# Order and due times of the row scatters in a planned attention and mixture-of-experts kernel

## The chip, the cores and the metric

The kernel runs on one core of one Trainium2 chip. The metric is device time in microseconds (us), the median of three runs.

## The reference

Eight batches of eight heads, 576 tokens, head size 64, with a causal window of 128 and a linear bias per head; then a mixture of eight experts on the 4608 resulting tokens (512 wide, 1024 hidden), each token going to one expert.

```
scores = q @ k.T / 8 + slope[h] * -|i - j|      where 0 <= i - j < 128, else -1e9
x      = (softmax(scores) @ v)                  -> (4608, 512)
logits = (x / |x|) @ (emb / |emb|).T / tau
e      = argmax(logits);  g = softmax(logits)[e]
out    = g * (relu(x @ w1[e]) @ w2[e])
```

## The kernel before, in words

**Two stages.** `attention` makes the tokens tile by tile, and `moe` runs the experts. There are 36 tiles of 128 query rows: per pair of batches eight tiles of one batch (a `first` one, which has no earlier tile, and three `full` ones, for each of the two batches) and one `pair` tile with the last 64 rows of both. Each tile is done in two halves of four heads, so that there are 72 half tiles, u = 0 to 71.

**A half tile** goes through TensorE (`score`, L595 and L616), VectorE (`merge` L626, `max` L633), ScalarE (`exp` L640), TensorE again (`flip`, a transpose, L648), ScalarE and VectorE (`phi` L494 and `plo` L497, which split the probabilities into two 16-bit parts), GpSimd (`mask`, two or three selects, L668 and L681; none in a `first` tile), TensorE (`av`, L700 and L716) and VectorE (`recip` L732, `norm` L738). A tile then has `xhi` (L752 or L754), `xlo` (GpSimd, L765), a transposing DMA of SyncE (`xdma`, L769), `logit` (L775, L779) and `lcopy` (L788). `v_lo` (L570) is a further GpSimd job per tile.

**Routing.** `GROUPS` is 8, 8, 8, 6, 4, 2 tiles. When the last tile of a group has its logits, a chain of some 20 small operations, nearly all on VectorE (`route`, L843 to L865), finds each token's expert and its row there (`di`); `mark` writes the token's number and weight beside it (L876); and `put`, an indirect DMA of GpSimd (L880, L881), scatters a tile's 128 rows of 514 words from the tile `gx` into the table `xs` in HBM. There are 13 `gx` buffers (`XBUFS`), so that tile T + 13 can be written only when tile T is scattered.

**The head start.** After the third group (`GP` = 2, 24 tiles) the expert that has most tokens is chosen (`head_ops`, L336 to L343). Its weights come in 16 pieces (`fetch` L927) that ScalarE and VectorE split (`whi` L930, `wlo` L934), its first 384 rows come from `xs` (`head_rows`, L941 and L945, which wait for the 24 scatters), and TensorE computes them between the attention's jobs (`hid` L962, `out` L986). `y` (L993 on ScalarE, L995 on VectorE) and `yput` (GpSimd, L998 and L396) store the result.

**The hand-over.** After the last group `count_ops` (L354 to L357) read how many tokens the head expert has in all, and `rank_ops` (L376 to L389) order the others. In `moe`, `blank_rows` (L1285) writes zeros from `zrow` behind an expert's last token, and `rows` (L1302, L1307, L1314) reads the expert's tokens from `xs` by a transposing DMA, which waits for all 36 scatters. `hidden` (L1391), `hidden_part`, `output` (L1435), `scaled` and `put` (L396) follow, expert by expert in the order of `TURNS`.

**Who sets the order.** The class `Plan` holds jobs with an engine, an assumed length in ns, what they come after, which buffers they take, and a due time. It gives each engine's next place to the job with the earliest due among those that can start within `SLACK` of the earliest start (400 ns on GpSimd); jobs marked `fill` come last. The due time of a stage of half tile u is 2800 u plus a constant (`STEP`, `DUE`): 5600 for `mask`, 16700 for `put`. The result is a fixed order of instructions on each engine, and on the chip an engine takes them in that order. An `ORDER` dependency only sets the order and makes nothing wait on the chip.

Of the kernel before, what the change touches and what calls it, by code (L numbers as in the profile page):

```python
# [39 lines left out]
GP = 2  # L40
# [128 lines left out]
def kernel(  # L169
# [156 lines left out]
    def head_ops(z):  # L326
# [5 lines left out]
        def ke(nm):  # L332
# [10 lines left out]
            ("DVE", 90, lambda: V.tensor_copy(k1("he", I32), k1("hf"))),  # L343
            ("SP", 500, lambda: head_box["start"]()),
        ]

    def count_ops(z):
        V = nc.vector

        def ke(nm):  # L350
            return kt_(nm, [P, E])

        return [
            ("DVE", 90, lambda: V.tensor_copy(ke("cnt"), z["cnt"])),  # L354
            ("DVE", 90, lambda: V.tensor_tensor(ke("hn"), ke("ho"), ke("cnt"), op=ALU.mult)),
            ("DVE", 90, lambda: V.tensor_reduce(kt_("n0", [P, 1]), ke("hn"), axis=AX.X, op=ALU.add)),
            ("DVE", 90, lambda: V.tensor_copy(kt_("n0i", [P, 1], I32), kt_("n0", [P, 1]))),  # L357
        ]

    def rank_ops(z):  # L360
# [42 lines left out]
    def attention(actx):  # L403
# [386 lines left out]
        def route_ops(gi):  # L790
# [47 lines left out]
            def ids():  # L838
# [22 lines left out]
                *(count_ops(z) if tail else []),  # L861
# [32 lines left out]
        def route_kinds(gi):  # L894
            G, tail = groups[gi], gi == len(groups) - 1
            o = [("DVE", 70), ("ACT", 100), ("ACT", 100)] + [("DVE", 70)] * 6 + [("DVE", 135)] * 7
            o += [("PE", 40 * G + (40 * G if tail or gi == GP else 0))]
            o += [("DVE", 90)] if gi == GP else []
            o += [("DVE", 90)] * 4 if tail else []
# [51 lines left out]

        def head_hidden(ft, c):
# [37 lines left out]
        def head_y(a):  # L990
            hd["y", a] = y = stg.tile([P, DM], F32, tag="stg", name=f"y_head_{a}")
            if a % 2:
                nc.scalar.activation(y, hd["ps2", a], AF.Copy, scale=hd["gs"][:, a : a + 1])  # L993
            else:
                nc.vector.tensor_scalar(y, hd["ps2", a], hd["gs"][:, a : a + 1], None, op0=ALU.mult)  # L995
# [45 lines left out]
        for T in range(NT):  # L1041
# [3 lines left out]
            for n in "kq":  # L1045
                if T >= 2:
# [9 lines left out]
                    f"turn_{n}{T}", "PE", 470 + SWITCH, lambda a=key: prep_pe(a[1], a[0]),  # L1056
# [20 lines left out]
            for hf in range(2):  # L1077
# [5 lines left out]
                    f"score{u}", "PE", (640 if first else 980 if pair else 960 if t % 2 else 1180) + 150, lambda a=a: score_pe(*a),  # L1083
# [4 lines left out]
                for j in range(2):  # L1088
# [16 lines left out]
                    f"flip{u}", "PE", 452 + SWITCH, lambda a=a: probs_pe(*a), after=[f"exp{u}_0", (f"exp{u}_1", -230)],  # L1105
# [16 lines left out]
                    f"av{u}", "PE", (490 if first else 1190 if pair else 842) + SWITCH, lambda a=a: values_pe(*a),  # L1122
# [16 lines left out]
                f"xhi{T}", "DVE" if dv else "ACT", 335 if dv else 520, lambda T=T: x_act(T),  # L1139
# [34 lines left out]
        for gi, G in enumerate(groups):  # L1174
# [6 lines left out]
            for i, (e, ns) in enumerate(kinds[0]):  # L1181
                dep = list(prev)
                if i == R_RANK and gi:
                    dep.append(f"total{gi - 1}")
                J(
                    f"route{gi}_{i}", e, ns, of(gi, 1, i), after=dep, due=due("route", u) + 150 * i,
# [10 lines left out]
            for g in range(G):  # L1197
# [5 lines left out]
                    f"put{T0 + g}", "POOL", 1030, of(gi, 3, g), land=1000, moves=700, after=[done, f"mark{T0 + g}", f"xlo{T0 + g}"], uses=[("gx", T0 + g)],  # L1203
                    due=due("put", u) + 1500 * g,
# [8 lines left out]
            if tail:  # L1213
                prev = [done]
                for i, (e, ns, f) in enumerate(rank_ops({})):
                    J(f"order{i}", e, ns, f, after=prev, due=due("route", u) + 150 * (i + 30))
                    prev = [f"order{i}"]
# [3 lines left out]
        for i in range(NP):  # L1221
# [4 lines left out]
            J(f"wlo{i}", "DVE", 602, lambda i=i: part_lo(i), after=[f"whi{i}"], uses=[("stg", i)], due=d + 5500, fill=True)  # L1226
        J("head_rows", "SP", 5500, head_rows, land=1500, moves=5000, after=[f"put{T}" for T in range(GT)] + [started], due=due("put", u) + 12000)
        J("head_info", "DVE", 150, head_info, after=["head_rows"], due=1e7)
# [10 lines left out]
        for a in range(HEAD // P):  # L1239
# [6 lines left out]
            J(f"y{a}", "ACT" if a % 2 else "DVE", 600, lambda a=a: head_y(a), after=[f"out{a}_5", "head_info"] + [f"fetch{i}" for i in range(NP)], makes=[("stg", ("y", a))], uses=[("ps2", a)], due=2e7)  # L1246
            J(f"yput{a}", "POOL", 1200, lambda a=a: head_put(a), after=[f"y{a}"], uses=[("y", a)], due=3e7)
# [9 lines left out]
    def moe(mctx):  # L1257
# [18 lines left out]
        def blank_rows(s):  # L1276
            (nb, hb), b0 = blocks(s), first_row(s) // P
            if s == 0:
                e = head_box["e"]
            else:  # L1280
                e = nc.sync.value_load(ebi[0:1, s : s + 1], min_val=0, max_val=E - 1)
            nt = sel_["n0i"][0:1, 0:1] if s == 0 else nki[0:1, s : s + 1]
            n = nc.sync.value_load(nt, min_val=0, max_val=NTOK)
# [8 lines left out]
            if s == 0:  # L1292
                state[s].update(w1=(w["w1h"], w["w1l"]), w2=(w["w2h"], w["w2l"]))
# [184 lines left out]
        for p, s in enumerate(TURNS):  # L1478
# [5 lines left out]
                f"blank{s}", "SP", 5.9 * ((nb - b0) * P + hb), lambda s=s: blank_rows(s), due=lead - 3000, early=handed["order"],  # L1484
# [3 lines left out]
                f"rows{s}", "SP", 7.0 * (SLOTS[s] - b0 * P) + 600, lambda s=s: rows(s), after=[(f"blank{s}", 2000)], early=handed["rows"],  # L1488
# [200 lines left out]
```

## Time and profile before

| what | us |
|---|---|
| median of three runs | 671.62 |
| lowest and highest of them | 667.55, 672.62 |
| the profiled execution, its own time | 668.15 |
| its span, first to last instruction | 666.4 |
| TensorE busy in the span | 629.3 |
| VectorE, ScalarE, GpSimd busy | 388.4, 331.3, 262.6 |
| mean granted TensorE clock | 0.985 |

The span is what the profile's rows divide up; 1.75 us of the execution's time lie around it. Matmuls are pipelined and their ends are modelled, so that a busy TensorE is not one at its peak. Times in rows count from the start of the span. The attention fills the span up to about 297 us, the experts the rest.

### The profile page before, as it was taken

Reading aid. Unit: us, or ns where it says so; the run is one execution under the profiler, and the core shown is the slowest. Engines: PE = TensorE matmul, PEld = TensorE weight load, DVE = VectorE, ACT = ScalarE, POOL = GpSimd, SP = SyncE. Lnnn points to the kernel's source line nnn. Section 1 sums busy time; section 2 is a strip of 40 time slices with the busy share of each in tenths; the row PEclk is TensorE's granted clock in tenths of the full one; section 3 lists DMA queues with packets and bytes.
Section 4 is the critical chain, followed back from the end, with each engine's and each line's share of the span. In section 5 each row is a group of like instructions: output and inputs, shape, how many; then the busy total and the mean of one; then the engine's idle time right before and its main releaser. Section 6 shows DMA issues by size and latency. Waiting matters only on the chain. (4 is left out here: it accounts for less than half of the span.)

```text
span 666.4 us, 15711 instructions
## 1 busy us (share of the span) xinstructions
PE 629.3 (94%) x6043; PEld 423.5 (64%) x6043; DVE 388.4 (58%) x989; ACT 331.3 (50%) x777; POOL 262.6 (39%) x472
## 2 busy tenths in 40 slices
PE   7999989989999998989989999999999999999993
PEld 4887767767877775636555585574674855754442
DVE  5988869997999999732356336245352364310250
ACT  5999777878877895302265225243332253210200
POOL 7677588779668656730110301011102012002011
PEclk9999999999988997999999999999999999999998
DMA  9998979988969993459999917807729264001000
GB/s 194 197 203 171 184 202 158 183 195 198 189 128 272 208 212 96 137 157 221 242 319 281 326 69 158 272 33 199 262 61 303 95 168 156 2 16 48 12 32 32
DMA packets 217676, 109.83 MB, mean 165 GB/s; under 512 B 195829, under 2 KB 195829, under 8 KB 217600
## 3 DMA queue, kind: packets, MB, share of 16 engines
q1 hardware_dynamic: 211760, 89.89, 61.2%
q0 software_dynamic: 5840, 18.92, 7.6%
q8 instruction: 48, 0.79, 0.5%
q14 instruction: 28, 0.23, 0.1%
HBM read 61.92 MB, written 28.12 MB: 135 GB/s over the span
## 5 line engine op out<-in xcount | busy, mean ns | idle before, releaser
L1391 PE MATMUL ps<-xT,w1h 128*128 128x272 f16 (+7 forms) x896 | 173.5, 293 | 5.2 <-DMA xT<-xs 3.2
L1391 PE MATMUL ps<-xT,w1l 128*128 128x272 f16 (+7 forms) x448 | 131.5, 293 | 0.0
L396 POOL DMA_INDIRECT out_dram<-y,ids x32 | 35.0, 1095 | 204.9 <-DVE y L1449 96.0
L1391 PEld LDWEIGHTS <-w1h 128*128 128x128 f16 x896 | 87.6, 98 | 35.9 <-issue 5.9
L1399 DVE SCALAR_TENSOR_TENSOR hl<-ps,hh 128x272 f16<-128x272 f32 (+7 forms) x112 | 51.5, 474 | 95.6 <-ACT hh L1401 95.6
L1435 PE MATMUL ps<-w2h,hl 128*128 128x512 f16 (+1 forms) x264 | 98.4, 373 | 1.4 <-DVE hl L1399 1.4
L1435 PE MATMUL ps<-w2h,hh 128*128 128x512 f16 (+1 forms) x264 | 98.4, 373 | 0.0
L1435 PE MATMUL ps<-w2l,hh 128*128 128x512 f16 (+1 forms) x264 | 98.4, 373 | 0.0
L1401 ACT ACTIVATE hh<-ps 128x272 f16<-128x272 f32 (+7 forms) x112 | 45.6, 425 | 101.7 <-PE ps L1391 92.2
L640 ACT ACTIVATE pe<-sc,nm 128x128 f32<-128x128 f32 x288 | 85.6, 390 | 12.9 <-DVE nm L633 9.9
L1435 PEld LDWEIGHTS <-hh 128*128 128x128 f16 x528 | 51.4, 98 | 58.6 <-issue 0.8
L616 PE MATMUL sc<-kh,qh 64*128 64x128 f32 (+2 forms) x768 | 69.8, 328 | 0.8 <-ACT qh L494 0.8
L494 ACT ACTIVATE pq<-ptp 128x512 f16<-128x512 f32 x72 | 55.1, 765 | 14.7 <-PE ptp L648 13.7
L616 PEld LDWEIGHTS sc<-kh,qh 64*128 64x128 f32 (+1 forms) x768 | 55.1, 183 | 9.2 <-issue 4.8
L497 DVE SCALAR_TENSOR_TENSOR pq<-ptp,pq 128x512 f16<-128x512 f32 x72 | 52.8, 733 | 11.5 <-ACT pq L494 11.0
L1366 DVE SCALAR_TENSOR_TENSOR w2l<-ws,w2h 128x1024 f16<-128x1024 f32 x28 | 33.8, 1223 | 38.0 <-ACT w2h L1368 37.7
L633 DVE TENSOR_REDUCE nm<-sc 128x2 f32<-128x256 f32 x144 | 55.2, 413 | 0.4 <-PE sc L616 0.3
L1366 DVE SCALAR_TENSOR_TENSOR w1l<-ws,w1h 128x1024 f16<-128x1024 f32 x28 | 33.4, 1221 | 37.0 <-ACT w1h L1368 36.8
L648 PE MATMUL ptp<-ident,pe 128*128 128x128 f32 x288 | 47.9, 288 | 5.7 <-ACT pe L640 2.2
L1391 PEld LDWEIGHTS <-w1l 128*128 128x128 f16 x448 | 43.8, 98 | 14.4
L1368 ACT ACTIVATE w2h<-ws 128x1024 f16<-128x1024 f32 x28 | 29.1, 1054 | 43.2 <-DMA ws<-moe_w_dram 41.0
L1368 ACT ACTIVATE w1h<-ws 128x1024 f16<-128x1024 f32 x28 | 28.4, 1052 | 44.1 <-DMA ws<-moe_w_dram 44.1
(231 smaller groups left out, 1203.9 us busy)
## 6 DMA issues: line engine op xcount, KB each, us to landing
ws<-moe_w_dram SPq DMA_DIRECT2D x56, 512.0 KB, 9.9
ldk<-k_dram SPq DMA_DIRECT2D x32, 256.0 KB, 4.5
ldq<-q_dram SPq DMA_DIRECT2D x32, 256.0 KB, 5.0
ldv<-v_dram SPq DMA_DIRECT2D x32, 256.0 KB, 4.2
stg<-moe_w_dram SPq DMA_DIRECT2D x16, 256.0 KB, 4.6
xs<-zrow SPq DMA_DIRECT2D x3, 1092.2 KB, 9.2
xs<-zrow SPq DMA_DIRECT2D x1, 1413.5 KB
xs<-zrow SPq DMA_DIRECT2D x1, 1285.0 KB
```

The source lines that it names most:

```text
L494: nc.scalar.activation(hi, ps, AF.Copy, scale=scale)
L497: nc.vector.scalar_tensor_tensor(lo, ps, scale, hi, op0=ALU.mult, op1=ALU.subtract)
L616: nc.tensor.matmul(sc[T, hf, j][o, l, w], qT[T]["h"][rows, hp, o], at["h"][rows, hp, kc], start=False, stop=True, skip_group_check=True,)
L633: nc.vector.tensor_reduce(nm_t[T, hf, j], sc[T, hf, j][:, :, 0:P], axis=AX.X, op=ALU.min)
L640: nc.scalar.activation(pr_t[T, hf][:, 2 * l + j, :], ps[:, l, 0:P], AF.Exp, bias=nm[:, l : l + 1], scale=-1.0)
L648: nc.tensor.transpose(pt[:, i, :], pe[:, i, :], ident)
L1366: nc.vector.scalar_tensor_tensor(lo_, x, SW, hi, op0=ALU.mult, op1=ALU.subtract)
L1368: nc.scalar.activation(hi, x, AF.Copy, scale=SW)
L1391: nc.tensor.matmul(ps[:, :w], a[:, kt, fs], xx[:, b + kt, c0 : c0 + w], start=(n == 0), stop=(n == len(jobs) - 1))
L1399: nc.vector.scalar_tensor_tensor(hl[:, ft, c0 : c0 + w], ps[:, :w], 0.0, hi, op0=ALU.max, op1=ALU.subtract)
L1401: nc.scalar.activation(hi, ps[:, :w], AF.Relu)
L1435: nc.tensor.matmul(ps, x[:, ft, a * P : (a + 1) * P], w[:, ft, c], start=(n == 0), stop=(n == len(jobs) - 1))
```

## The change

The due time of the scatters is new. For the first two groups it is the due time of the mask just before tile T + 13 needs the buffer; for the third it is that of the masks 58 to 65; for the last three groups it lies behind all masks, and they also come after `head_blank`. `head_blank` is a new job of SyncE that writes the zero rows of the head expert behind its count after the third group, so that the late scatters write over them; `count_ops` and the first `blank_rows` are gone, and `head_ops` has one more cast (`hmi`). The copy of the counts that opened `count_ops` is now the first of `rank_ops`. `yput` comes after the last scatter in GpSimd's order, and all three `y` are on ScalarE. Many assumed lengths in the plan are set anew.

```diff
+            ("DVE", 90, lambda: V.tensor_copy(k1("hmi", I32), k1("hm"))),
-    def count_ops(z):
...
+            ("DVE", 90, lambda: V.tensor_copy(ke("cnt"), z["cnt"])),
-                *(count_ops(z) if tail else []),
+        def head_blank():
+            n = nc.sync.value_load(sel_["hmi"][0:1, 0:1], min_val=HEAD, max_val=NTOK)
+            m = (SLOTS[0] + 31) // 32 * 32 - HEAD
+            d = nc.sync.dma_start(
+                xs[ds(hd["e"], 1), ds(n, m), :].rearrange("o (a p) c -> p (o a) c", p=32),
+                zrow[0:32].unsqueeze(1).to_broadcast([32, m // 32, ROW]),
+            )
+            for p_ in scatters:
+                tc.declare_no_dep(d.ins, p_.ins, reason="rows beyond the expert's tokens")
         def head_y(a):
-            if a % 2: nc.scalar.activation(...)
-            else: nc.vector.tensor_scalar(...)
+            nc.scalar.activation(y, hd["ps2", a], AF.Copy, scale=hd["gs"][:, a : a + 1])
-  turn, flip  "PE", 470 + SWITCH, 452 + SWITCH
+  turn, flip  "PE", 470 + SWITCH // 2, 452 + SWITCH // 2
-  score  (640 if first else 980 if pair else 960 if t % 2 else 1180) + 150
+  score  (960 if first else 1078 if pair else 1185 if t % 2 else 1212) + SWITCH
-  av     (490 if first else 1190 if pair else 842) + SWITCH
+  av     (500 if first else 1720 if pair else 870) + SWITCH // 2
-  xhi    335 if dv else 520
+  xhi    400 if dv else 535
-  route  ns
+  route  ns + (45 if e == "DVE" else 0)
-  wlo    602
+  wlo    750
-  J(f"put{T0 + g}", "POOL", 1030, ..., after=[done, f"mark{T0 + g}", f"xlo{T0 + g}"],
-    due=due("put", u) + 1500 * g)
+  J(f"put{T0 + g}", "POOL", 1270, ..., after=[...] + (["head_blank"] if gi > GP else []),
+    due=due("mask", 2 * (T0 + g + XBUFS) - 2) if gi < GP else due("mask", u + 11 + g) if gi == GP
+        else due("mask", 2 * NT) + 1e4 + 100 * g)
+  J("head_blank", "SP", 1300, head_blank, land=1500, moves=2300,
+    after=[started] + [(f"put{T}", ORDER) for T in range(GT)] + then("score", 2 * NT - 8),
+    due=due("put", u) + 20000)
-  J(f"y{a}", "ACT" if a % 2 else "DVE", 600, ...)
-  J(f"yput{a}", "POOL", 1200, lambda a=a: head_put(a), after=[f"y{a}"], ...)
+  J(f"y{a}", "ACT", 600, ...)
+  J(f"yput{a}", "POOL", 1200, lambda a=a: head_put(a), after=[f"y{a}", (f"put{NT - 1}", ORDER)], ...)
   def blank_rows(s):
       if s == 0:
-          e = head_box["e"]
+          state[s] = dict(e=head_box["e"], ...); return
-  J(f"rows{s}", ..., after=[(f"blank{s}", 2000)], ...)
+  J(f"rows{s}", ..., after=[(f"blank{s}", 2000 if s else ORDER)], ...)
```

## Rows read from the trace of the kernel before

**Rows 1.** The profile's page, part 1: busy time, share of the span and instructions of each engine.

```profile
PE 629.3 (94%) x6043; PEld 423.5 (64%) x6043; DVE 388.4 (58%) x989; ACT 331.3 (50%) x777; POOL 262.6 (39%) x472
```

**Rows 2.** Busy time in stretches: the stretch, its length, then busy us and instructions of PE, PEld, DVE, ACT and POOL, the granted clock, the DMA share and GB/s.

```profile
30.00:70.00 40.00, 40.00 (x612) 32.28 (x608) 33.72 (x97) 35.77 (x98) 30.41 (x44) 1.00 1.00 184
90.00:100.00 10.00, 7.62 (x98) 5.77 (x98) 4.74 (x14) 7.52 (x22) 9.04 (x16) 1.00 0.91 259
150.00:160.00 10.00, 8.53 (x143) 6.73 (x140) 7.73 (x21) 7.90 (x25) 9.63 (x15) 1.00 0.87 229
190.00:200.00 10.00, 8.88 (x110) 6.78 (x106) 9.90 (x39) 6.46 (x17) 6.92 (x21) 0.83 0.51 110
210.00:220.00 10.00, 8.39 (x102) 6.67 (x100) 9.07 (x21) 7.78 (x20) 7.93 (x13) 0.83 1.22 234
240.00:258.00 18.00, 14.76 (x229) 11.34 (x226) 18.00 (x57) 15.19 (x42) 11.05 (x14) 0.99 0.76 150
260.00:270.00 10.00, 10.00 (x89) 6.45 (x86) 8.45 (x23) 4.50 (x13) 8.23 (x15) 0.78 0.35 132
```

**Rows 3.** TensorE in order of time: the first matmuls of the scores of half tiles u = 6, 18, 24, 36, 48, 54 and 66. Columns: start, length, engine, line, what it writes and reads.

```profile
26.12 0.39 PE L595 MATMUL sc<-brow,bcol 64*128 64x512 bf16 x2
...
64.20 0.38 PE L595 MATMUL sc<-tab_first,identb 128*128 128x256 bf16 x2
...
85.46 0.39 PE L595 MATMUL sc<-brow,bcol 64*128 64x512 bf16 x2
...
128.16 0.38 PE L595 MATMUL sc<-tab_first,identb 128*128 128x256 bf16 x2
...
170.96 0.39 PE L595 MATMUL sc<-brow,bcol 64*128 64x512 bf16 x2
...
190.92 0.38 PE L595 MATMUL sc<-tab_first,identb 128*128 128x256 bf16 x2
...
236.06 0.39 PE L595 MATMUL sc<-brow,bcol 64*128 64x512 bf16 x2
```

**Rows 4.** GpSimd in order of time, the first group's scatters: the first and the sixth, and the first selects of the masks of half tiles 22 and 23 behind them.

```profile
86.72 1.18 POOL L881 DMA_INDIRECT xs<-gx,di  x1 [1.06 <-DVE nm L633]
...
93.27 0.96 POOL L881 DMA_INDIRECT xs<-gx,di  x1 [0.19 <-issue]
94.25 0.64 POOL L668 TENSOR_SCALAR_AFFINE_SELECT md<-pq 128x512 f32<-128x512 f32 x1
...
97.95 0.64 POOL L668 TENSOR_SCALAR_AFFINE_SELECT md<-pq 128x512 f32<-128x512 f32 x1
```

**Rows 5.** VectorE in order of time: the `plo` of half tiles 22, 23 and 70, each the last thing that its mask needs.

```profile
86.67 0.75 DVE L497 SCALAR_TENSOR_TENSOR pq<-ptp,pq 128x512 f16<-128x512 f32 x1
...
89.39 0.72 DVE L497 SCALAR_TENSOR_TENSOR pq<-ptp,pq 128x512 f16<-128x512 f32 x1
...
263.61 0.74 DVE L497 SCALAR_TENSOR_TENSOR pq<-ptp,pq 128x512 f16<-128x512 f32 x1
```

**Rows 6.** TensorE in order of time: the `av` that uses the mask of 94.25 us, with its wait in brackets.

```profile
94.94 0.21 PE L716 MATMUL av<-vh,md 128*128 128x65 f16 x1 [1.22 <-POOL md L668]
```

**Rows 7.** The scatters and the split of the head's weights (shortest, median and longest ns, first and last start), and two rows of the list of DMA issues (KB each and us from issue to landing, where given).

```profile
L881 POOL DMA_INDIRECT xs<-gx,di x36: 957/963/1182, 86.7 to 290.1; - x36
...
L934 DVE SCALAR_TENSOR_TENSOR w1l<-stg,w1h x8: 676/756/2341, 209.7 to 230.3; 128x512 f16<-128x512 f32 x8
...
xs<-zrow SPq DMA_DIRECT2D x1, 578.2 KB, 4.5
xs<-gx,di POOLq DMA_INDIRECT x36, 5.4
```

**Rows 8.** The last rounds of the attention, in order of time on GpSimd, VectorE, SyncE and TensorE: the first select of mask 70; the head's first `yput`; the last scatter; the copy of the counts (the first of `count_ops`), the head's first `y` and the last group's rows `di`; the blank rows of the head expert and the first `rows`; the head's last matmul and the experts' first.

```profile
269.65 0.90 POOL L681 TENSOR_SCALAR_AFFINE_SELECT tails<-pq 64x256 f32<-64x256 f32 x2
...
287.54 1.00 POOL L396 DMA_INDIRECT out_dram<-y_head,ids_head  x1 [1.29 <-DVE df L864]
...
290.11 0.96 POOL L881 DMA_INDIRECT xs<-gx,di  x1 [0.19 <-issue]
...
285.70 0.14 DVE L354 COPY cnt<-ptr 128x8 f32<-128x8 f32 x1
...
286.51 0.75 DVE L995 TENSOR_SCALAR y_head<-ps_head,gs_head 128x512 f32<-128x512 f32 x1
...
287.68 0.17 DVE L865 CAST di<-df 128x2 int32<-128x2 f32 x1
...
287.34 0.38 SPq L1285 DMA_DIRECT2D xs<-zrow  x1
295.33 2.26 SPq L1302 DMA_TRANSPOSE xT<-xs  x1
...
296.45 0.38 PE L986 MATMUL ps_head<-w2h,hl_head 128*128 128x512 f16 x1
300.07 0.40 PE L1391 MATMUL ps<-xT,w1h 128*128 128x288 f16 x2 [3.23 <-DMA xT<-xs]
```

**Rows 9.** SyncE and TensorE in order of time: the read of the head expert's rows, a load for the last tile, and the head's first matmuls.

```profile
228.30 4.20 SPq L941 DMA_TRANSPOSE x_head<-xs  x1
...
242.07 1.32 SPq L428 DMA_DIRECT2D ldq<-q_dram  x2
...
243.30 0.49 PE L962 MATMUL ps_head<-x_head,w1h 128*128 128x384 f16 x2
```

More of the change, by code (lines that the diff above doesn't have):

```diff
@@ L1202, in attention @@
                 J(
-                    f"put{T0 + g}", "POOL", 1030, of(gi, 3, g), land=1000, moves=700, after=[done, f"mark{T0 + g}", f"xlo{T0 + g}"], uses=[("gx", T0 + g)],
-                    due=due("put", u) + 1500 * g,
+                    f"put{T0 + g}", "POOL", 1270, of(gi, 3, g), land=1000, moves=700, after=[done, f"mark{T0 + g}", f"xlo{T0 + g}"] + (["head_blank"] if gi > GP else []), uses=[("gx", T0 + g)],
+                    due=due("mask", 2 * (T0 + g + XBUFS) - 2) if gi < GP else due("mask", u + 11 + g) if gi == GP else due("mask", 2 * NT) + 1e4 + 100 * g,
                 )
@@ L1214, in attention @@
                 prev = [done]
-                for i, (e, ns, f) in enumerate(rank_ops({})):
-                    J(f"order{i}", e, ns, f, after=prev, due=due("route", u) + 150 * (i + 30))
+                for i, (e, ns, _) in enumerate(rank_ops({})):
+                    J(
+                        f"order{i}", e, ns, lambda i=i, gi=gi: rank_ops(box[gi][0])[i][2](), after=prev, due=due("route", u) + 150 * (i + 30),
+                        uses=[] if i else [key],
+                    )
                     prev = [f"order{i}"]
@@ L1225, in attention @@
             J(f"whi{i}", "ACT", 520, lambda i=i: part_hi(i), after=[f"fetch{i}"], uses=[("stg", i)], due=d + 5000, fill=True)
-            J(f"wlo{i}", "DVE", 602, lambda i=i: part_lo(i), after=[f"whi{i}"], uses=[("stg", i)], due=d + 5500, fill=True)
+            J(f"wlo{i}", "DVE", 750, lambda i=i: part_lo(i), after=[f"whi{i}"], uses=[("stg", i)], due=d + 5500, fill=True)
         J("head_rows", "SP", 5500, head_rows, land=1500, moves=5000, after=[f"put{T}" for T in range(GT)] + [started], due=due("put", u) + 12000)
+        J(
+            "head_blank", "SP", 1300, head_blank, land=1500, moves=2300, after=[started] + [(f"put{T}", ORDER) for T in range(GT)] + then("score", 2 * NT - 8),
+            due=due("put", u) + 20000,
+        )
         J("head_info", "DVE", 150, head_info, after=["head_rows"], due=1e7)
@@ L1245, in attention @@
                 )
-            J(f"y{a}", "ACT" if a % 2 else "DVE", 600, lambda a=a: head_y(a), after=[f"out{a}_5", "head_info"] + [f"fetch{i}" for i in range(NP)], makes=[("stg", ("y", a))], uses=[("ps2", a)], due=2e7)
-            J(f"yput{a}", "POOL", 1200, lambda a=a: head_put(a), after=[f"y{a}"], uses=[("y", a)], due=3e7)
+            J(f"y{a}", "ACT", 600, lambda a=a: head_y(a), after=[f"out{a}_5", "head_info"] + [f"fetch{i}" for i in range(NP)], makes=[("stg", ("y", a))], uses=[("ps2", a)], due=2e7)
+            J(f"yput{a}", "POOL", 1200, lambda a=a: head_put(a), after=[f"y{a}", (f"put{NT - 1}", ORDER)], uses=[("y", a)], due=3e7)
         handed["free"], end = plan.run(dict(FREE))
@@ L1483, in moe @@
             J(
[L1484 removed]
+                f"blank{s}", "SP", 5.9 * ((nb - b0) * P + hb) if s else 0, lambda s=s: blank_rows(s), due=lead - 3000, early=handed["order"] if s else 0.0,
                 after=before(f"rows{TURNS[p - 1]}") if p else [],
```

38 lines of the change are left out of this document (11 added, 27 removed).

## The prediction

> **What bounds the kernel now.** I read the page's busy times first: TensorE is busy in 94% of the span, no other engine in more than 58% [rows 1]. So a stall counts only where TensorE waits. The table of stretches shows where. From 30 to 70 us TensorE has no gap at all, with VectorE at 33.72 of 40 and GpSimd at 30.41 of 40; from 90 to 100 and from 150 to 160 it has 7.62 and 8.53 of 10, while GpSimd has 9.04 and 9.63; from 240 to 258 it has 14.76 of 18, with VectorE full at 18.00 [rows 2]. Two different engines hold it up, then, at different places.
>
> The pace puts a price on it. Twelve half tiles without routing or scatters (u = 6 to 18) take 64.20 - 26.12 = 38.08 us. Those behind the first group's end (24 to 36) take 42.70, those around the second's (36 to 48) 42.80, and those around the third's (54 to 66) 45.14: 4.62, 4.72 and 7.06 too much [rows 3].
>
> The order on GpSimd shows why. The first group's scatters start at 86.72 and six of them run to 94.23, 1.31 us apart (6.55 over five). Behind them stands the mask of half tile 22, which starts at 94.25 [rows 4], although its last input was ready at 86.67 + 0.75 = 87.42 [rows 5]; mask 23 starts at 97.95 and could at 90.11. They are 6.8 and 7.8 us late, and TensorE's `av` says in brackets that it waited for that select [rows 6].
>
> **The change part by part.** *Scatters of the first three groups.* Nothing is removed: 24 scatters of 1.31 us stay on GpSimd, but they come due one per tile (third group: one per half tile) instead of all ahead of the masks. Not all the lost pace is theirs. The half tiles 18 to 24 take 85.46 - 64.20 = 21.26 us for six, 19.04 at the undisturbed pace, and no scatter has begun yet [rows 3, 4]: 2.22 us are the routing chain's. The second and third groups' stretches hold their chains too. In the third, one split of the head's weights took 2341 ns where the shortest took 676 [rows 7]; I take these 1.67 us off as well. The scatters' share is 4.62 + (4.72 - 2.22) + (7.06 - 2.22 - 1.67) = 10.3 us.
>
> How much comes back? At the undisturbed pace GpSimd is busy 30.41 / 40 = 76% without scatters, 28.95 us in twelve half tiles; six scatters more make 36.8 of 38.08, or 97%. So it is nearly full, each scatter can still put 1.3 us ahead of a mask, and whenever the plan's clock and the chip's differ, TensorE waits a little. Bounds: nothing comes back, or all 10.3. I take 55%, since the load just fits under TensorE's pace: 5.7 us.
>
> *Late scatters and the hand-over.* The experts' first matmul starts at 300.07, 3.23 us after the head's last one ended at 296.83. It waits for rows whose read SyncE issued at 295.33, 5.2 us after the last scatter began at 290.11; the median landing of a scatter is 5.4 us [rows 7, 8]. What stands ahead of that scatter goes: the four counting operations (VectorE, 285.70 to 286.34: 0.64 us), a `y` between two links of the chain that makes `di` (286.51 to 287.18 when the next link starts: 0.67 us), and a `yput` which ended at 288.54 and let the last two scatters go at 288.84, where `di` was there at 287.85 (0.9 us). Together 2.2 us, so the gap becomes 1.0. The ten late scatters of the fourth and fifth group take 13.1 us. They stood between mask 69 and the last group's `di` before, too: the same work in another order, so they should fit, and if they don't, the gap grows by what is over. Mask 70 started at 269.65, 5.3 us after its input at 264.35 [rows 5, 8], behind six scatters that now stand behind it. This lets the last tile's chain come earlier, but TensorE has head work to fill that time, so I count it at nothing: bounds 0 and the 1.0 us of gap that is left.
>
> *Blank rows.* The old blank's 578 KB were issued at 287.34 and needed 4.5 us, so they landed at 291.8, before the last scatter at about 295.5 [rows 7, 8]: taking them off that path is worth 0. The new one has the same size, comes after score 64 and is waited for by the late scatters on GpSimd, with masks queued behind them. Since those scatters are due behind all masks, some 30 us cover the 4.5. Without that cover a mask would be 4.5 us late, which I keep as a bound.
>
> *Assumed lengths.* They reorder every engine and no row shows the result. For a scatter (1030 to 1270, where rows show 1.31 us) and for the split (602 to 750, median 756) they come nearer to the rows. The bound is the loss in the stretch where VectorE is full, 18 - 14.76 = 3.24 us, either way [rows 2]; I take 0. The cast `hmi` and the three `y` on ScalarE stand on no path that I can find: between 0 and one `y` of 0.75 us, taken as 0.
>
> The sum is 5.7 + 2.2 = 7.9 us, against 668.15 in the profiled execution: 660.2. That execution is 3.5 below the median of the runs, so I put the gain on the mean of all four executions, (667.55 + 672.62 + 671.62 + 668.15) / 4 = 670.0, and forecast **662**.
>
> **The rivals.** *VectorE or GpSimd takes the place of the masks.* VectorE needs 33.72 / 40 x 38.08 = 32.1 us per twelve half tiles, and is already full where routing and splitting come together, as at 240 to 258; GpSimd would be 97% busy. Against it: from 90 to 100 VectorE has 4.74 of 10, so that there it waited too [rows 2]. If a fifth of the 10.3 comes back, the gain is 2.1 + 2.2 = 4.3: 665.7.
>
> *Slower: the head's rows come too late.* The third group's scatters are due with the masks 58 to 65, and score 66 starts at 236.06 [rows 3]. If the last of them waits for its due, it lands at 241.5 or later, where the read of the head's rows is now issued at 228.30. SyncE takes its queue in order, and would hold the loads behind that read, such as the one at 242.07 for the last tile, by up to 8 us. The head work that TensorE begins at 243.30 could not fill the hole [rows 9]. That is 8 us lost against half of the recovery (2.8) and no gain at the hand-over: 675. It decides itself where the read is issued after 243. Against it, the plan puts a scatter wherever GpSimd would be idle, and GpSimd has 11.05 of 18 from 240 to 258 [rows 2].
>
> *More comes back.* All 10.3, the whole gap of 3.2, and the lower clock level: from 260 to 270 the granted clock is 0.78, which is 4.4 us at 1.2 instead of 2.4 GHz behind a stretch with idle TensorE [rows 2], worth up to 2.2. Together 15.7: 654.
>
> *Scatters stay in a row.* The plan starts what can start first, and a scatter in a short hole needs no due time. If the bursts stay, only the hand-over gains 2.2: 668. Against it, the masks' due times now stand ahead of the scatters'.
>
> *Scatters stretch beside VectorE.* In the bursts VectorE was partly idle; now scatters run beside its full load. They took 957 to 1182 ns, median 963 [rows 7]. If each of the 24 took the longest, that is 24 x 0.22 = 5.3 us more on an engine that is 97% full, and the gain is 2.6: 667.4. The Trainium skill (SBUF — State Buffer, "Who interferes with whom") speaks for this: a VectorE operation that uses both port pairs blocks GpSimd wholly, and a scatter's descriptors wait for it. The trace shows such a lock on VectorE's side, the split of 676 to 2341 ns, but none on a scatter beyond 0.22 us.
>
> **How the numbers follow.** Chances: forecast 0.45 (657 to 667), the next engine 0.20, slower 0.12, more 0.13, scatters in a row 0.05, stretched scatters 0.05. One per cent of 671.62 is 6.7 us, about what a measurement of this kernel can tell from no change, so the limits are 664.9 and 678.3. Faster: three quarters of the forecast (0.34), all of "more" (0.13) and 0.4 of the next engine (0.08), 0.55. Slower: half of the slower case, 0.06. The rest, 0.39, lies within. The range goes from 653 to 673: it leaves out half of the slower case and a little at the low end.
>
> **What would show it.** Right: no more than two scatters in a row before 260 us; masks 22, 23, 38 and 39 less than 2 us behind their `plo`; the half tiles 24 to 36 in about 40 us; TensorE's last gap near 1 us. Wrong: the pace unchanged with VectorE or GpSimd full in these stretches; the head's rows read after 243; a scatter that waits for the blank's landing with masks behind it; a gap at the hand-over over 3 us.

## The result and the profile after

The kernel before takes 669.42 us (median of 20 runs, 667.36 to 673.93), the changed one 674.12 (20 runs, 671.75 to 678.34). The ratio is 1.0059, 95% interval 1.0042 to 1.0076: some 4 us slower, where 8 faster were forecast. In three of the five sets of runs below the kernel before took 687 to 689 us instead of 669 to 670, once on a chip that gave 668.92 in another set, and why stays open: each ratio is to the kernel before in the same set, and one beside 687 to 689 tells more of that kernel than of an edit.

The profiled execution of the changed kernel took 676.36 us, its span 674.51. That is 8.1 us over the span before, while the medians differ by 4.7: the execution before lay 1.3 under its median, this one 2.2 over. The busy times are as before [rows 1]:

```profile
PE 633.9 (94%) x6043; PEld 424.5 (63%) x6043; DVE 386.6 (57%) x985; ACT 332.9 (49%) x779; POOL 264.2 (39%) x472
```

**The masks did come on time.** GpSimd and VectorE in order of time, to be read against [rows 4, 5]: scatters and the first selects of masks 22 and 23, then the `plo` of half tiles 22 and 23 (it starts the mask when it ends, 88.44 and 91.36).

```profile
87.83 1.18 POOL L869 DMA_INDIRECT xs<-gx,di  x1 [0.17 <-POOL spare L868]
89.02 0.65 POOL L657 TENSOR_SCALAR_AFFINE_SELECT md<-pq 128x512 f32<-128x512 f32 x1
...
91.60 0.63 POOL L657 TENSOR_SCALAR_AFFINE_SELECT md<-pq 128x512 f32<-128x512 f32 x1
...
93.02 0.99 POOL L869 DMA_INDIRECT xs<-gx,di  x1 [0.16 <-issue]
...
87.71 0.73 DVE L486 SCALAR_TENSOR_TENSOR pq<-ptp,pq 128x512 f16<-128x512 f32 x1
...
90.61 0.75 DVE L486 SCALAR_TENSOR_TENSOR pq<-ptp,pq 128x512 f16<-128x512 f32 x1
```

Masks 22 and 23 start 0.6 and 0.2 us behind their input, not 6.8 and 7.8. **The pace did not follow.** The score starts of half tiles 24, 36, 48, 54 and 66, against [rows 3]:

```profile
85.91 0.39 PE L584 MATMUL sc<-brow,bcol 64*128 64x512 bf16 x2
...
129.17 0.38 PE L584 MATMUL sc<-tab_first,identb 128*128 128x256 bf16 x2
...
171.44 0.39 PE L584 MATMUL sc<-brow,bcol 64*128 64x512 bf16 x2
...
191.09 0.38 PE L584 MATMUL sc<-tab_first,identb 128*128 128x256 bf16 x2
...
238.94 0.39 PE L584 MATMUL sc<-brow,bcol 64*128 64x512 bf16 x2
```

24 to 36 take 43.26 us (42.70 before), 36 to 48 take 42.27 (42.80), 54 to 66 take 47.85 (45.14). The stretches, with the columns of [rows 2]:

```profile
90.00:100.00 10.00, 9.80 (x162) 8.18 (x158) 8.62 (x23) 9.08 (x27) 9.27 (x15) 1.00 0.75 130
150.00:160.00 10.00, 9.93 (x143) 8.03 (x141) 9.31 (x25) 8.76 (x25) 9.51 (x16) 1.00 0.87 169
190.00:200.00 10.00, 8.23 (x122) 6.79 (x121) 9.93 (x37) 6.41 (x18) 7.03 (x19) 0.87 0.71 145
210.00:220.00 10.00, 7.17 (x81) 5.33 (x82) 7.02 (x18) 8.02 (x22) 7.76 (x12) 0.89 1.22 182
240.00:258.00 18.00, 16.44 (x258) 12.46 (x257) 18.00 (x51) 15.23 (x42) 11.41 (x14) 1.00 0.93 185
260.00:270.00 10.00, 8.52 (x95) 5.67 (x95) 7.35 (x32) 4.61 (x14) 4.64 (x14) 0.83 0.28 43
85.00:129.00 44.00, 40.95 (x602) 32.77 (x601) 36.48 (x104) 34.83 (x95) 36.70 (x59) 0.96 1.02 180
```

The holes have moved. 90 to 100 and 150 to 160 are full now, 210 to 220 and 260 to 270 are emptier, and over the whole stretch 85 to 129 TensorE is busy 40.95 of 44 us, where it was 40.66. What it waits for is new. That stretch before, then TensorE's longest waits in it before and after (us in all, times, the longest):

```profile
85.00:129.00 44.00, 40.66 (x612) 32.23 (x610) 36.04 (x104) 35.15 (x96) 36.60 (x57) 1.00 0.99 183
...
PE av L716 <- POOL md L668: 1.5, 2, 1.2
...
PE ptl L764 <- DMA xT<-gx: 2.3, 1, 2.3
```

In all its waits for GpSimd there, `av` lost 2.2 us before and loses 0.4 now. So the late masks did cost TensorE something, and the change took that away; a wait of the logits for their transposed tile `xT` came in its place. The granted clock adds to it. It is 0.96 in that stretch, 3.4 us at 1.2 instead of 2.4 GHz; it fell at 105.2 us, behind seven us (98 to 105) in which TensorE was busy for 4.46. In the second profile of the changed kernel, below, it stays at 1.00 and 24 to 36 take 42.16 us.

More on the logits' waits. First the logits of a tile, in TensorE's order; then SyncE's issue of the transposing DMA that they read; then the view of the tile `xT` up to 290 us, with who waited for that DMA and its shortest, median and longest time from issue to landing (as far as the profile gives it, for 17 of the 36).

```profile
217.39 0.26 PE L764 MATMUL ptl<-enc,xT 128*128 128x16 f16 x4 [2.35 <-DMA xT<-gx]
...
205.51 1.47 SPq L758 DMA_TRANSPOSE xT<-gx  x1
...
  PEld L764: 10.9, 8
  PE ptl L764: 8.2, 6
...
DMA to landing us min/median/max: 2.7/4.6/11.8
```

This transposed tile took from 205.51 to 217.34, with scatters from 200.5 to 208.2 and six loads of head weights from 202.0 to 204.7 beside it. TensorE's matmuls waited 8.2 us for such tiles; in the kernel before one wait of 0.3 us. There `xlo`, which precedes the transposing DMA, stood behind the scatters on GpSimd, so the DMA came after their traffic; now it runs beside it, while the plan goes on assuming a landing 1 us after issue. Of the 36 transposing DMAs 6 had a scatter beside them before (one that began up to 6 us ahead of the issue or 4 us behind it), and 14 have one now.

**The hand-over closed, and the experts stumbled.** The last scatter, the first `rows`, the head's last matmul, and the experts' first matmul with its gap, against [rows 8]:

```profile
292.38 0.97 POOL L869 DMA_INDIRECT xs<-gx,di  x1 [0.19 <-issue]
...
295.88 2.13 SPq L1301 DMA_TRANSPOSE xT<-xs  x1
...
302.05 0.38 PE L984 MATMUL ps_head<-w2h,hl_head 128*128 128x512 f16 x1
303.20 0.41 PE L1390 MATMUL ps<-xT,w1h 128*128 128x288 f16 x2 [0.78 <-ACT y_head L990]
```

The gap fell from 3.23 to 0.78 us. The rows' read did not come sooner for that: it was issued 0.55 us later than before (295.33), while the head's last matmul ended 5.60 us later (302.43 for 296.83). What is left of the wait is for ScalarE's `y`. And from that matmul to the end of the span it takes 371.31 us instead of 366.36. GpSimd, ScalarE and TensorE show why:

```profile
293.66 1.00 POOL L385 DMA_INDIRECT out_dram<-y_head,ids_head  x1 [0.19 <-issue]
...
300.56 0.19 POOL L1337 COPY ids<-info 128x2 int32<-128x2 int32 x1 [5.79 <-DMA info<-xs]
...
301.45 1.05 POOL L385 DMA_INDIRECT out_dram<-y_head,ids_head  x1 [0.49 <-issue]
...
313.55 0.18 POOL L1337 COPY ids<-info 32x1 int32<-32x1 int32 x1 [10.93 <-DMA out_dram<-y_head,ids_head]
...
314.41 1.06 POOL L385 DMA_INDIRECT out_dram<-y_head,ids_head  x1 [0.39 <-POOL gs L1338]
...
321.37 1.06 ACT L1367 ACTIVATE w1h<-ws 128x1024 f16<-128x1024 f32 x1 [14.62 <-DMA out_dram<-y_head,ids_head]
...
322.78 0.61 PE L1434 MATMUL ps<-w2h,hh 128*128 128x512 f16 x1 [6.37 <-ACT hh L1400]
```

The three scatters of the head's output (`yput`) now have the first expert's row numbers (`ids`) between them: the second half of `ids` waits for the second `yput` to land, and the third `yput` stands behind it. By these waits the memory that `ids` and ScalarE's first split write to was the head's `y`: the split waits for the third `yput` to land, and behind it on ScalarE stand the `hh` that TensorE needs. Before, all three went ahead of `ids` (287.5 to 297.9). Each of the two stages has a plan of its own, and neither sets the order of a `yput` against `ids`.

The head's rows were read at 243.5, not 228.3 [rows 9]. In SyncE's queue that read now stands behind the new blank rows (issued at 238.21) and waited 4.1 us for their landing; the last row is from the list of SyncE's waits.

```profile
243.51 3.28 SPq L928 DMA_TRANSPOSE x_head<-xs  x1
...
250.71 0.48 PE L960 MATMUL ps_head<-x_head,w1h 128*128 128x384 f16 x2 [0.33 <-ACT pe L629]
...
SPq L928 <- DMA xs<-zrow: 4.1, 1, 4.1
```

All nine profiles of the changed kernel, mended or not, have this wait (1.6 to 4.6 us); those of the hand-over's edits alone have none. The next transposing DMA is issued at 248.15. What the wait costs in the end was not measured apart.

Span against span, the 8.1 us are: up to u = 24 +0.45; 24 to 36 +0.56; 36 to 48 -0.53; 48 to 54 -0.31; 54 to 66 +2.71; 66 to the head's end +2.72; gap -2.45; experts +4.95. These are two single executions: in the second profile of the changed kernel, below, 24 to 36 take 1.1 us less and 54 to 66 take 2.0 us more, so only the larger parts say much.

### The profile page after: what moved, and what is told of

Its sections match the earlier page's. It is cut to its first block, busy times and chain, and to the rows that moved or that the text cites. A ratio compares the mean times of both kernels' runs of the same rounds, so it can differ in the third digit from the quotient of the medians.

```text
span 674.5 us, 15712 instructions
## 1 busy us (share of the span) xinstructions
PE 633.9 (94%) x6043; PEld 424.5 (63%) x6043; DVE 386.6 (57%) x985; ACT 332.9 (49%) x779; POOL 264.2 (39%) x472
## 5 line engine op out<-in xcount | busy, mean ns | idle before, releaser
L1398 DVE SCALAR_TENSOR_TENSOR hl<-ps,hh 128x272 f16<-128x272 f32 (+7 forms) x112 | 51.4, 474 | 105.2 <-ACT hh L1400 105.1
L629 ACT ACTIVATE pe<-sc,nm 128x128 f32<-128x128 f32 x288 | 84.1, 382 | 8.7 <-DVE nm L622 7.3
L605 PE MATMUL sc<-kh,qh 64*128 64x128 f32 (+2 forms) x768 | 71.9, 334 | 0.0
L705 PE MATMUL av<-vh,mp 128*128 128x65 f16 (+1 forms) x512 | 48.1, 198 | 2.7 <-POOL mp L657 2.3
```

Of the source, the lines that this page charges most:

```text
L605: nc.tensor.matmul(sc[T, hf, j][o, l, w], qT[T]["h"][rows, hp, o], at["h"][rows, hp, kc], start=False, stop=True, skip_group_check=True,)
L629: nc.scalar.activation(pr_t[T, hf][:, 2 * l + j, :], ps[:, l, 0:P], AF.Exp, bias=nm[:, l : l + 1], scale=-1.0)
L705: nc.tensor.matmul(o_, a_, b_, start=False, stop=(n == last), skip_group_check=True)
L1398: nc.vector.scalar_tensor_tensor(hl[:, ft, c0 : c0 + w], ps[:, :w], 0.0, hi, op0=ALU.max, op1=ALU.subtract)
```

## The experiments

The theory (1): the gain of the masks is taken by logits that wait for transposing DMAs, and the experts' start by a `yput` behind `ids`. Rivals: (2) the assumed lengths order the work worse as a whole; (3) spread scatters are dear in themselves.

### Each part of the change alone, in the kernel before

*The assumed lengths alone* (first set, before 670.22):

```diff
-  f"put{T0 + g}", "POOL", 1030, ...
+  f"put{T0 + g}", "POOL", 1270, ...
   (and the new lengths of turn, score, flip, av, xhi, route, wlo; old due times)
```

> The kernel before with the new assumed lengths of the plan alone (turn, score, flip, av, xhi, routing, scatter, weight split). Theory 1 (the loss comes from the scatters' new places and from the experts' start): within 2 us of the kernel before. Theory 2 (the figures order the work worse): 3 to 5 us over it. The prediction said 0, at most 3.2 either way.

Measured: 667.94 us, ratio 0.9961 (0.9940 to 0.9983), 2.6 us faster. Theory 2 falls, and the 2 us of theory 1 are passed by a little. Its first scores of half tiles 24 and 36, at 85.52 and 125.81, are 40.29 us apart where 42.70 were, and this with six scatters in a row ahead of mask 22, which starts 6.9 us late (mask 23: 7.7). GpSimd's first scatter, the sixth and that mask; VectorE's `plo` for it; then the stretch from 85 to 129:

```profile
87.43 1.18 POOL L881 DMA_INDIRECT xs<-gx,di  x1 [0.17 <-POOL spare L880]
...
93.97 0.96 POOL L881 DMA_INDIRECT xs<-gx,di  x1 [0.19 <-issue]
94.95 0.64 POOL L668 TENSOR_SCALAR_AFFINE_SELECT md<-pq 128x512 f32<-128x512 f32 x1
...
87.32 0.73 DVE L497 SCALAR_TENSOR_TENSOR pq<-ptp,pq 128x512 f16<-128x512 f32 x1
...
85.00:129.00 44.00, 43.10 (x654) 34.27 (x654) 38.41 (x109) 36.76 (x102) 38.12 (x59) 1.00 0.86 192
```

TensorE is busy 43.10 of 44 us behind a mask as late as ever, and waits 0.2 us for GpSimd in all: it had other work in its order. A late mask is not yet a stall. At the hand-over this kernel loses: the gap ahead of the experts is 6.75 us, where it was 3.23.

*The due times alone*:

```diff
-  due=due("put", u) + 1500 * g,
+  due=due("mask", 2 * (T0 + g + XBUFS) - 2) if gi < GP else due("mask", u + 11 + g) if gi == GP else due("mask", 2 * NT) + 1e4 + 100 * g,
```

> The kernel before with the scatters' new due times alone. Theory 1 (spread scatters do bring the masks on time, but logits then wait for transposes that run beside the scatters' and loads' traffic): masks of half tiles 22, 23, 38 and 39 under 2 us late, TensorE's waits for xT<-gx 4 us or more, the time within 2.5 us of the kernel before. Prediction's term: 5.7 us faster. Theory 3 (spreading is dear in itself): over 3 us slower, with few waits for xT<-gx.

> The scatters' new due times alone, again, on a chip where the kernel before takes 668 to 671 us. On the other chip half tiles 24 to 36 took 42.28 us, 36 to 48 44.51 and 54 to 66 48.29, and TensorE waited 1.7 us for xT<-gx. Prediction's term: 5.7 us faster. Theory 3 (spreading is dear in itself): over 3 us slower, the same stages long. Theory 1 as first put (logits wait for late transposes once the scatters are spread): within 2.5 us of the kernel before; since the waits were not there, it now needs the figures too.

> The scatters' new due times alone. If the kernel before takes 668 to 671 us on this chip: prediction's term 5.7 us faster; theory 3 over 3 us slower; theory 1 as now put (the new due times bring nothing there, since the plan lets other engines' waits take the masks' place) within 2.5 us. If it takes 687 again: 672 to 673, as in the two sets before.

> The scatters' new due times alone. Where the kernel before takes 668 to 671 us: the prediction's term says 664; since this kernel took 672.6 to 673.5 on two other chips, whose rows of scatters cost more, and since its half tiles 36 to 48 and 54 to 66 are longer there than in the kernel before here (45 against 42.80, 47.5 against 45.14), we now expect 671 to 674, that is 1 to 4 us slower. Where the kernel before takes 687 or more: 672 to 674 again.

Measured: 673.53 (before 687.41, ratio 0.9798, 0.9767 to 0.9829), 672.65 (688.61; 0.9775, 0.9748 to 0.9801), 673.04 (689.47; 0.9766, 0.9740 to 0.9792), and in the last set 668.58 (668.92; 0.9988, 0.9971 to 1.0006). Beside a kernel before of 668.92 us the due times bring nothing that can be told from zero, neither the 5.7 us of the prediction nor theory 3's loss; my last expectation, drawn from the other sets, was wrong as well. Theory 1's waits of 4 us or more did not come either: TensorE's matmuls waited 0.3, 0.2, 0.0 and 3.3 us for `xT` in the four profiles, so spread scatters alone do not bring the 8.2. In the last run the masks 22, 23 and 24 started 1.7 to 1.8 us behind their input, and 24 to 36 still took 44.00 us (granted clock 0.96; at 1.00, in the other three, 42.03 to 42.45). What holds the pace there once the masks are on time stays open. And the hand-over's gap closed in these runs too, though the counting operations were still in place. The experts' first matmul of the last run, with the head's end at 300.04, 3.2 us later than before, and the rows' read issued at 294.95:

```profile
300.89 0.42 PE L1391 MATMUL ps<-xT,w1h 128*128 128x288 f16 x2 [0.85 <-DVE y_head L995]
```

*The hand-over's edits alone* (figures and due times as before):

```diff
-  *(count_ops(z) if tail else []),
-  J(f"y{a}", "ACT" if a % 2 else "DVE", ...);  J(f"yput{a}", ..., after=[f"y{a}"], ...)
+  J(f"y{a}", "ACT", ...);  J(f"yput{a}", ..., after=[f"y{a}", (f"put{NT - 1}", ORDER)], ...)
+  J("head_blank", "SP", 1300, head_blank, ...)
```

> The kernel before with the hand-over's edits alone (no count chain, y on ScalarE only, its scatters behind the rows' last, blank rows early); figures and due times as before. On GpSimd the head's third scatter stands behind the first expert's row numbers here too, but behind both of them and right after. Theory 1: the gap ahead of the first expert matmul falls from 3.2 to about 1, ScalarE's wait at the first weight split stays under 10 us, and the time is 1 to 2.5 us under the kernel before. Prediction's term: 2.2 faster. Rival (one of these edits itself starts the stall of ScalarE): wait over 13 us, 2 to 4 us slower than the kernel before.

> The hand-over's edits alone, again, on a chip where the kernel before takes 668 to 671 us. Prediction's term: 2.2 faster. Theory 1: 1 to 2.5 us faster, gap ahead of the first expert matmul about 1 us, experts' part 366 to 368 us. Rival: 2 us or more slower, with ScalarE's wait at the first weight split over 13 us.

> The hand-over's edits alone. Where the kernel before takes 668 to 671 us: 1 to 2.5 us faster by theory 1 and by the prediction's term (2.2). Where it takes 687 or more: 1 to 3 us slower than it, as twice before, with the gap ahead of the experts at 1.3 to 1.6 us.

Measured: 689.97 (before 687.41; 1.0047, 1.0027 to 1.0068), 690.45 (688.61; 1.0029, 1.0010 to 1.0049), 673.09 (668.92; 1.0058, 1.0035 to 1.0080). Slower each time, 3.9 us in the last set; the prediction's 2.2 faster and my own theory for it fall. In the last run's profile (an execution of 670.30, under that median) the gap fell to 1.52 us, but the head ends at 299.50 instead of 296.83, and the experts take 367.56. Two rows show one wait on the way to that later end: TensorE's matmul with values of the last tile, and the split of these values on GpSimd, now behind a mask:

```profile
256.40 0.19 PE L705 MATMUL av<-vo,md 128*128 128x64 f16 x1 [1.78 <-POOL vo L559]
...
254.79 1.56 POOL L559 TENSOR_TENSOR vo<-ldv,vh 128x512 f16<-128x512 f32 x1
```

Half tiles 66 to 71 took 26.37 us there (22.22 before). ScalarE's longest wait for a `yput` is 8.3 us, not 13: with both halves of `ids` ahead of the third `yput`, nothing waits long between them. Which of the hand-over's edits moved that split, and what the rest of the 3.9 us is, these runs don't say. One step did get shorter by these edits. From the last scatter's start to the issue of the rows' read it takes 3.2 to 3.7 us in all twelve profiles of kernels that have them, and 4.7 to 5.2 in the seven of kernels with all 36 scatters and without them.

*The changed kernel again*, in the set where the kernel before took 687.41:

> The changed kernel itself, timed beside the parts of it on one chip. Every theory: 673 to 675 us, a ratio of 1.004 to 1.008 to the kernel before. Its second profile is to show which of the first one's figures repeat: theory 1 expects TensorE's waits for xT<-gx at 5 us or more and ScalarE's wait of over 13 us at the first expert's weight split again, and half tiles 24 to 36 and 54 to 66 over 41 and 47 us.

Measured: 674.83 us, as before; but the ratio there is 0.9799 (0.9767 to 0.9832). The expected ratio failed with the kernel before, not with this one. The second profile repeats the waits: its logits waited for `xT` (10.9 us by that view, TensorE's weight loads counted with it; 19.1 in the first), the experts took 371.21, and 54 to 66 took 49.89 (granted clock 0.86, where the first had 0.93).

### Two single mends in the changed kernel

*Logits later*: one figure of the plan, so that logits stand later in TensorE's order.

```diff
-  f"xdma{T}", "SP", 1320, lambda T=T: x_dma(T), land=1000, moves=1350, ...
+  f"xdma{T}", "SP", 1320, lambda T=T: x_dma(T), land=4000, moves=1350, ...
```

> The changed kernel with one figure of the plan altered: a transposing DMA is assumed to land 4000 ns after its issue instead of 1000, so that the logits stand later in TensorE's order. Theory 1 (the masks' gain was given back by logits that wait for transposes running beside scatters): TensorE's waits for xT<-gx in the window 0:262 fall from 7.9 us to under 3, the attention part ends 3 to 5 us sooner, and the time is 3 to 5 us under the changed kernel. Theory 2 (the new assumed lengths order the work worse as a whole): within 1.5 us of the changed kernel. Theory 3 (scatters spread among the masks are dear in themselves): within 1.5 us too, with the pace of half tiles 24 to 36 still at 43.

> The later logits alone. Theory 1: 6 to 8 us under the changed kernel (674), that is 666 to 668, and the experts' part still 371 us. Theory 2': as e18.

Measured: 666.30 (before 670.22; 0.9943, 0.9921 to 0.9965) and 669.58 (689.47; 0.9714, 0.9690 to 0.9738). Of the first, who waited for `xT`, and two stretches:

```profile
  PEld L764: 1.9, 3
  PE ptl L764: 1.3, 3
...
85.00:129.00 44.00, 42.88 (x666) 34.36 (x662) 38.87 (x108) 37.79 (x104) 38.97 (x63) 1.00 1.01 193
210.00:220.00 10.00, 9.81 (x150) 7.59 (x150) 9.68 (x27) 10.00 (x27) 9.03 (x17) 1.00 1.21 209
```

The wait falls from 8.2 to 1.3 us, TensorE fills 42.88 of 44 and 9.81 of 10, 24 to 36 take 39.83 us, 54 to 66 take 43.60. The forecast "about 40 us" was within reach; another figure of the plan stood in the way. The experts still take 371.43. Another length in a plan reorders much, so that this alone does not show that all of the 7.8 us are the logits' waits; these fell by 6.9.

*The third `yput` first*:

```diff
   ins = nc.gpsimd.tensor_copy(i_, info[pr, bl, 0].bitcast(I32))
+  if s == 0:  # order on GpSimd alone, no wait
+      tc.add_manual_dep(ins.ins, out_sc[-1].ins.name, DependencyInfo(NoSync, DATA), ...)
```

> The changed kernel with one order set by hand: on GpSimd the first expert's row numbers stand behind the head's last scatter to the output, as in the kernel before. Theory 1 (5 us of the loss are ScalarE's wait for a scatter of the head that stood behind those numbers): ScalarE's wait of 14.6 us at its first weight split falls under 8, the stretch from the first expert matmul to the end falls from 371.3 to about 366.5 us, and the time is 4 to 5 us under the changed kernel, that is level with the kernel before within 1.5. Rival (the experts' start is late for another reason, the hand-over itself): within 1.5 us of the changed kernel.

> The head's last scatter ahead of the first row numbers, alone. Theory 1: 4 to 7 us under the changed kernel, 667 to 670, the experts' part 366 to 368 us, and TensorE still waits 5 us or more for xT<-gx.

Measured: 666.79 (before 670.22; 0.9961, 0.9937 to 0.9984) and 670.03 (689.47; 0.9721, 0.9697 to 0.9746). The experts' part is 367.93 and 365.64 us. GpSimd's third `yput` and `ids`, and ScalarE's first split, of the first:

```profile
299.92 0.98 POOL L385 DMA_INDIRECT out_dram<-y_head,ids_head  x1 [4.07 <-ACT y_head L990]
300.90 0.21 POOL L1337 COPY ids<-info 128x2 int32<-128x2 int32 x1
...
311.20 1.06 ACT L1374 ACTIVATE w1h<-ws 128x1024 f16<-128x1024 f32 x1 [7.96 <-DMA out_dram<-y_head,ids_head]
```

The split starts at 311.20 instead of 321.37, and TensorE's wait of 6.37 us is gone. Elsewhere every engine's instructions stand in the order of the changed kernel. The ratios 1.0059 and 0.9961 make it 6.6 us, of which the experts' part holds 3.4 in the first profile and 5.7 in the second. 4.1 us between the first profile and that of the changed kernel lie ahead of score 66, where nothing was altered: so much can two executions of one order differ.

*Both mends*:

> The changed kernel with both mends: the transposing DMA assumed to land after 4000 ns, and the head's last scatter ahead of the first expert's row numbers on GpSimd. Theory 1 (two separate losses, one in the attention part and one at the experts' start): they add up; 3.5 to 7 us under the run with the later logits alone, that is 659 to 663 us and a ratio of 0.984 to 0.990. Theory 2' (what both runs gained is one and the same, the plan's order being chancy by some 4 us): 665 to 668 like either alone.

> The changed kernel with both mends again, since in the set before this one the kernel before itself took 687 us on that chip and all rows of scatters cost more there. Theory 1 (two separate losses): where the kernel before takes 668 to 671 us, a ratio of 0.984 to 0.991, under those of either mend alone (0.9943 and 0.9961). Theory 2' (both mends hit one and the same loss): 0.994 to 0.997.

> The changed kernel with both mends, beside each alone on one chip. Theory 1 (two separate losses that add up): its time is under either mend alone by 2.5 us or more. Theory 2' (one and the same loss): within 1.5 us of the better one.

Measured: 663.46 (before 687.41; 0.9654, 0.9624 to 0.9684), 667.38 (688.61; 0.9688, 0.9638 to 0.9737), 664.47 (689.47; 0.9626, 0.9604 to 0.9649). The last set has each mend alone, 669.58 and 670.03 us: together they are 5.1 and 5.6 us under these, twice the 2.5 that theory 1 asked. These are two separate losses. Against the changed kernel's 0.9799 the three ratios are -0.85%, -0.78% and -1.73%, a full sum, but 0.9799 is of another set. The first run missed its 659 to 663 us by 0.5. The ratios expected (0.984 to 0.990, then 0.984 to 0.991) were for a kernel before of 668 to 671 us; no such set has both mends, so they are not tested.

### Two controls

*No scatters of the first two groups*, to price them: the order of everything else is that of the kernel before. Eight DMAs blank those rows at the start, which delays the first score to 28.83 us, so the total (690.51 us; 1.0284, 1.0246 to 1.0322) says nothing, but the stages do.

```diff
   nc.gpsimd.memset(spare, 0.0)
+  if gi < GP:
+      return
   ins = nc.gpsimd.indirect_dma_start(xs_rows[:, :], ...)
```

> The kernel before without the scatters of the first two groups (16 of 36; their rows of the experts' table are blanked by eight DMAs at the start instead, so the output lacks those tokens); the order of everything else is the same. The prediction's term (the scatters cost 2.4 us in half tiles 24 to 36 and 2.5 in 36 to 48, the routing 2.2 each): 24 to 36 take about 40.3 us and 36 to 48 about 40.3. Rival (the pace there is set by the routing and the engines' own work, the masks' lateness is mostly beside other work): 42 to 43 as before. Half tiles 54 to 66, whose scatters stay, serve as control: 45.1 as before, within 0.7. Theory 1 expects something between, about 41 each.

The first matmuls of the scores 24, 36 and 48:

```profile
112.38 0.39 PE L599 MATMUL sc<-brow,bcol 64*128 64x512 bf16 x2
...
152.34 0.27 PE L599 MATMUL sc<-tab_first,identb 128*128 128x256 bf16 x1
...
193.78 0.39 PE L599 MATMUL sc<-brow,bcol 64*128 64x512 bf16 x2
```

24 to 36 take 39.96 us (2.74 less), 36 to 48 take 41.44 (1.36 less), the control 45.73 (45.14 before). The expectation above has the prediction's term wrong: for the first group the prediction put 4.62, the routing's 2.22 being taken off for the second and third alone. So its 4.62 + 2.50 = 7.1 measure 4.1: 2.74 and 1.36, a little over half of each.

*Logits later in the kernel before*:

```diff
-  ... land=1000, moves=1350, ...   (the kernel before)
+  ... land=4000, moves=1350, ...
```

> The kernel before with the one figure of the plan altered: the transposing DMA assumed to land after 4000 ns. Theory 1 (logits wait for transposes only since the change, because there the transposes run beside the scatters; in the kernel before they waited 0.3 us in all): within 2 us of the kernel before. Rival (the figure is worth 7 us in any order): 5 us or more faster than the kernel before, and then what it gives to the changed kernel is no give-back of the change.

Measured: 684.98 (before 688.61; 0.9966, 0.9938 to 0.9994), 2.3 us faster, a little over what theory 1 allowed and under half of the rival's 5. To the changed kernel the same figure gives 7.8 us by the ratios 1.0059 and 0.9943, and 5.9 by 0.9799 and 0.9714, which like this control stand beside a kernel before of 687 to 689. So some 2 us of it are worth having in any order, and the rest, 3.5 us or more, gives back what the change lost. Beside a kernel before of 669 us this control is missing.

## Why the prediction was wrong

- **What bounds the kernel: right engine.** TensorE's waits decide, as said, and it did wait 2.2 us for late masks from 85 to 129 us. But "the order on GpSimd shows why" holds for that one order of TensorE: with the masks equally late, other assumed lengths alone brought 24 to 36 to 40.29 us.
- **"The scatters' share is ... 10.3 us": too much.** For the first two groups it holds 7.1, and without their scatters these stretches are 4.1 shorter. The third group's 3.17 was not measured.
- **"I take 55%: 5.7 us": failed, and this decides.** The part that came back by moving the scatters is 0.8 us (-0.4 to 1.9) alone, and in the whole change none: 24 to 36, 36 to 48 and 54 to 66 take 2.7 us more together. The reason given, that GpSimd's load just fits, was beside the point. GpSimd had room (36.70 of 44 us busy), the masks came on time, and TensorE's order had new waits: 2.3 us for `xT` from 85 to 129, where 2.2 for the masks went.
- **The rival "the next engine takes the place" was the nearest, with the wrong name.** Not VectorE or GpSimd but a DMA did, by the logits that wait for it. The prediction followed the scatters on GpSimd and not what stood behind them there, `xlo` and the transposing DMA. That these going sooner, into the scatters' traffic, is the whole of it is not shown: with the due times alone, whose scatters are spread as much, the waits are 0 to 3.3 us, not 8.2.
- **Hand-over gap 3.23 to 1.0: right in the number (0.78), by luck.** The steps named were to bring the rows' read 2.2 us forward. It came 0.55 us later, and the gap closed because the head's end came 5.60 us later; the due times alone, without any of these steps, closed it to 0.85. **"Together 2.2 us" as gain: failed.** The edits alone cost 3.9 us (2.3 to 5.4), most of it unexplained.
- **What the experts lost (4.95 us in the profile) has no term.** The nearest is "the cast `hmi` and the three `y` on ScalarE stand on no path that I can find", taken as 0. The three `yput`s began between 287.5 and 297.9 us before and between 293.7 and 314.4 after, and the experts' first split waits for their landing. The prediction priced a `yput` only as something ahead of the last scatters, and did not ask what waits for it. That the two share memory stood in no row that I had read.
- **Blank rows at 0**: not separated from the other edits of the hand-over, but two things speak against 0, though no mask waits for the new blank. The step from the last scatter to the rows' read is some 1.6 us shorter where the old blank is gone, and SyncE's read of the head's rows waits 4.1 us for the new one, which the prediction expected to hold up scatters and masks alone.
- **Assumed lengths at 0, bound 3.24**: 2.6 faster alone, inside the bound. But the sum of parts, -2.6 - 0.8 + 3.9 = 0.5, is not the whole (3.9): the parts are not independent, since the plan orders everything anew. The 3.4 us between have an interval of some 2.6 either way. The logits' waits fit them in size, 8.2 us in the changed kernel where the figures, the due times and the hand-over alone show 1.5, 3.3 and 1.0; which pair makes them was not run.
- **The slower rival (head's rows after 243, 675 us)**: its condition came true (243.51) and the time lies near, but its price does not. From score 66 to the head's end it lost 2.7 us, not 8, and the later-logits kernel, which reads the rows at 235.8, has the same experts' loss.
- **Scatters in a row, stretched scatters**: neither. No more than three stand in a row before 260 us (two were named). The scatter's median is 986 ns against 963 [rows 7], the longest 1179: the rule drawn from the Trainium skill (SBUF — State Buffer, "Who interferes with whom") has no visible price here. Which of VectorE's operations use both port pairs no row tells, and that the split of 2341 ns was such a lock is not shown.

## What to carry to other kernels

In a kernel ordered by a plan, an operation that ends its wait sooner also starts its successors sooner: follow what stands behind the moved operation to its DMA, and check that the plan's landing time holds in the traffic that it will meet. Price a late buffer by the idle time of the engine that uses it, never by its own lateness. And when a tail is reordered, list who inherits its buffers: a scatter that was harmless at 298 us cost some 5 us at 314 because the next stage's first split was waiting for its memory.

## What the runs showed of the hardware

A transposing DMA took 2.7 to 11.8 us to land (median 4.6 of 17), where 3.7 was the median and 7.8 the longest of 21 before. A scatter of the head's output that was issued within 2 us of the first load of the experts' weights took 11.1 to 11.7 us to land, in the profiles of five kernels; in the kernel before the last one landed (301.08) ahead of that load (301.32) and took 3.2. The issue of a scatter on GpSimd kept its length meanwhile, 963 ns in a row and 986 spread.
